# Query-key products added on VectorE before one mask matmul, gate bias and residual put into PSUM by ScalarE

## The chip, the cores and the metric

One core of one Trainium2 chip. A core has TensorE (PE, matrix products out of SBUF into PSUM, eight banks of 512 fp32 per partition), VectorE (DVE), ScalarE (ACT), GpSimd (POOL) and SyncE (SP), each with a queue of its own that runs in order, and DMA engines that move data. The metric is device time in microseconds (us) of one execution, the median of several runs. All matrix operands are bf16.

## What is computed

With S = 2048 tokens and D = 512 features, `xn` is the layernorm of `x`, and the output is `x + A(xn) + B(xn)`:

```python
# A: 32 heads of 16 features; every token looks at 8 keys, 2 tokens apart
q, k, v = split(xn @ wqkv)                       # wqkv [512, 1536]
logits[h,s,w] = sum_d q[h,s,d]*k[h,s-2*w,d] * 16**-0.5   # w = 0..7, masked where s-2w < 0
attn = softmax(logits, over w)
A = concat_h(sum_w attn[h,s,w]*v[h,s-2*w]) @ wo  # wo [512, 512]
# B: gMLP with a spatial gate
z = gelu(xn @ w_in)                              # w_in [512, 1792]
z1, z2 = z[:, :896], layernorm(z[:, 896:])
g = w_sp @ z2 + b_sp[:, None]                    # w_sp [2048, 2048]
B = (z1 * g) @ w_out                             # w_out [896, 512]
```

## The kernel before

The program is a list of tasks. Each names its engine, what it reads and writes, and an estimated duration. A planner (`Plan.schedule`, line 94) then plays the tasks through in estimated time, picks for each engine the task that can begin earliest (and among those within 120 ns the one of better class and earlier place in the list), and so fixes the order of each engine's queue before anything runs. Tasks with `prio=FILL` are of a lower class: they fill gaps. Waits between engines are derived from reads and writes, overlapping buffers included: two names for the same place in the SBUF "arena" wait for each other. On the chip every queue keeps the planned order, whatever the real durations are. A task that must wait holds up all that stands behind it in its queue.

Tokens are taken in 16 blocks of 128 (b) and 4 column groups of 512 (j or tc).

*First stage, up to about 78 us of the profile.* `ln_block` (623) normalises a block and transposes it into `xnT`, by PE for the first four and by DMA on SP for the others. `z2_block` (826) makes the second half of z with a gelu on ACT; `z2_sq` and `z2_wave` normalise it (a power on POOL, line 880, and four multiplies on DVE, 883). `v_block` (669) makes the values, which POOL's DMA writes to a scratch tensor in device memory. `qk_pair` (686, matmuls at 694) makes Q and K, transposed, 128 features by 512 tokens, for one of four chunks c of features: chunk c holds features 128c to 128c+127, that is eight heads of 16. ACT copies both out of PSUM (702).

*Attention weights.* `prod_reduce` (713) is called for each j and c. DVE multiplies Q with the eight shifted views of K (720) into a product buffer of 128 x 4096, one of four. After the fourth chunk, 32 matmuls (733) with a 0/1 mask `E8` as stationary operand add up the 16 features of every head. Each uses 32 of the 128 columns of the array, so four run side by side in different column groups, and the four chunks are accumulated in PSUM (banks 6 and 7, `psl`). The mask has 128 columns, 32 for each chunk, and is made on POOL by one memset and eight selects (542 to 550). `softmax` (755) takes maximum and difference out of PSUM on DVE (763, 765) and, after every second j, an exponential on ACT (782) for two j; `softmax_tail` (787) does sums, reciprocal and transposes on DVE.

*z1.* `z1_group` (845, matmuls at 851) makes the first half of z, 28 groups, with a gelu on ACT (856), into `z1T`.

*Gate.* `g_group(fc, tc)` (947) takes one of 7 chunks of 128 features and one tc: 16 matmuls (956) with the transposed spatial weights `wT`, in one of four banks. DVE then adds the bias (963, PSUM to `tg` in SBUF) and multiplies `z1T` by the result in place (966). The spatial weights come in by a transposing DMA on SP (`ld_wT`, 888), in two slots of 2 MB: the one for tc = 0 after the first stage, that for tc = 1 only after the first two value loads (1058), the others when a slot is free.

*Values.* `pv_block(b)` (971): DVE multiplies the gathered values by the attention weights (999, 128 x 4096) and adds eight terms down to one in three steps (1001, 1004, 1007). The result lies in one of two buffers `On`, and a transposing DMA on SP (1010) puts it into `OT`. The values come from the scratch tensor through ACT's queue (983) into two buffers `Ve`.

*Output.* `out_block(tb)` (1016): four matmuls with `wo` (1031) and seven with `w_out` (1035) into one of banks 4 to 7; DVE adds the residual (1041), which ACT's queue has loaded (1022); ACT's queue stores the result (1045). The last block is cut into 384 and 128 columns.

The outer loop (1052) lists, for every tc, the gate groups, the value blocks, and the output blocks of tc - 1.

In the arena, `OT` has a place of its own; `Ve`, the product tiles `Vs`, `On`, `xres` (residual) and `yout` all lie over Q, K and the product buffers; the two `wT` slots lie over input, Q, K and V weights and the V buffers.

Of the kernel before, what the change touches and what calls it, by code (L numbers as in the profile page):

```python
# [14 lines left out]
class Plan:  # L15
# [276 lines left out]
ALU = mybir.AluOpType  # L292
# [11 lines left out]
    fill=1,  # L304
# [5 lines left out]
def build_kernel(nc, A_x, A_wqkv, A_wo, B_x, B_w_in, B_w_sp, B_b_sp, B_w_out, out, report=False, sched_kw=None,  # L310
# [33 lines left out]
    NPB = 4 if R2 else 2  # L344
# [9 lines left out]
    base += 4 * S  # L354
# [5 lines left out]
    off["tg"] = base + FC * 512 + 2048  # L360
# [5 lines left out]
    g3_a = 4 * 512 * NQ + ksz + NPB * 4096  # L366
    off["Ve"] = base
    off["Vs"] = base + (9216 if VEXT else 0)
    off["On"] = off["Vs"] + NVS * 4096
    off["xres"] = off["On"] + 1024  # L370
    off["yout"] = off["xres"] + 2048
    base += max(g3_a, off["yout"] + 2048 - base)
# [22 lines left out]
    with ExitStack() as es:  # L395
# [46 lines left out]
        for s_ in range(2):  # L442
            R1(("On", s_), "On", 512, 512 * s_)
            R1(("tg", s_), "tg", 512, 512 * s_)
# [78 lines left out]
        def setup_masks():  # L523
# [17 lines left out]
            else:  # L541
                T("pool", lambda g: g.memset(A("E8", 128), 1.0), reads=[("rstd", 3)], writes=["E8"], est=150, name="E8a", prio=2)
                for c in range(4):
                    eo = AC(off["E8"] + 32 * c, [[1, 32]])
                    T("pool", (lambda eo, c: lambda g: g.affine_select(
                        out=eo, in_=eo, pattern=[[-16, 32]], compare_op=ALU.is_ge, fill=0.0, base=128 * c,
                        channel_multiplier=1))(eo, c), writes=["E8"], est=250, name="E8b%d" % c, prio=2)
                    T("pool", (lambda eo, c: lambda g: g.affine_select(
                        out=eo, in_=eo, pattern=[[16, 32]], compare_op=ALU.is_ge, fill=0.0, base=15 - 128 * c,
                        channel_multiplier=-1))(eo, c), writes=["E8"], est=250, name="E8c%d" % c, prio=2)  # L550
# [135 lines left out]
        def qk_pair(j, c):  # L686
            k = next_pair()
            for which in range(2):
                col0 = which * 512 + 128 * c

                def mm(t, col0=col0, which=which):
                    last = None
                    for dc in range(4):
                        last = t.matmul(bank(k + which), AC(off["wqk"] + 1024 * dc + col0, [[1, 128]]),  # L694
                                        AC(off["xnT"] + dc * S + 512 * j, [[1, 512]]), start=(dc == 0),
                                        stop=(dc == 3))
                    return last
# [13 lines left out]
        pb_ctr = [0]  # L711

        def prod_reduce(j, c):
            s_ = pb_ctr[0] % NPB
            pb_ctr[0] += 1
            qb = AC(q_off(c, j), [[0, 8], [1, 512]])
            kb = AC(k_off(c, j), [[-2, 8], [1, 512]])
            pbv = AC(off["pb"] + 4096 * s_, [[512, 8], [1, 512]])
            rd = [("QT", c, j), ("KT", c, j), ("KT", c, j - 1) if j > 0 and not R2 else ("KTpad", c, j)]
            T("dve", lambda v: v.tensor_tensor(pbv, qb, kb, ALU.mult), reads=rd, writes=[("pb", s_)],  # L720
              est=c_dve(4096, 2.0), name="prod%d_%d" % (j, c), prio=FILL)

            if R2:
                if c < 3:
                    return

                def mm(t):
                    last = None
                    for wh in range(2):
                        for cc in range(4):  # L730
                            sc = (s_ - 3 + cc) % NPB
                            for g in range(4):
                                last = t.matmul(  # L733
                                    PC(32 * g * PR + 3072 + 512 * wh, [[1, 512]], 32),
                                    AC(off["E8"] + 32 * cc, [[1, 32]]),
                                    AC(off["pb"] + 4096 * sc + 2048 * wh + 128 * g, [[512, 4], [1, 128]]),
                                    start=(cc == 0), stop=(cc == 3))
                    return last
                T("pe", mm, reads=[("pb", i) for i in range(4)] + ["E8"], writes=["psl"],
                  est=8 * 232.0 + 190, name="red%d" % j, margin=cfg.get("m_red", 800.0))  # L740
                return

            def mm(t):
                last = None
                for blk in range(4):
                    t0, ts = tok(4 * j + blk)
                    for w in range(8):
                        last = t.matmul(ps[:, 3072 + blk * 256 + w * 32 + 8 * c: 3072 + blk * 256 + w * 32 + 8 * c + 8],
                                        AC(off["pb"] + 4096 * s_ + 512 * w + t0 - 512 * j, [[ts, 128]]), E8,
                                        start=True, stop=True)  # L750
                return last
            T("pe", mm, reads=[("pb", s_), "E8"], writes=["psl"], est=32 * 25 + 30, name="red%d_%d" % (j, c),
# [141 lines left out]
        for j in range(NJ):  # L894
# [24 lines left out]
            for c in range(4):  # L919
                prod_reduce(j, c)  # L920
# [7 lines left out]
        ld_wT(0)  # L928
        for j in range(NJ):
# [17 lines left out]
        def g_group(fc, tc):  # L947
            k = gcnt[0] % 4
            ts_ = gcnt[0] % 2
            gcnt[0] += 1  # L950
            r_ = tc % NWS

            def mm(t):
                last = None
                for sh in range(NB):
                    last = t.matmul(bank(k), AC(off["z2"] + FH * sh + 128 * fc, [[1, 128]]),  # L956
                                    AC(off["wT"] + WSL * r_ + sh * 512, [[1, 512]]), start=(sh == 0),
# [4 lines left out]
            tgv = A("tg", 512, 512 * ts_)  # L962
# [155 lines left out]
```

## Time and profile before

| | us |
|---|---|
| median of 3 runs | 245.22 (245.14 to 245.85) |
| profiled execution, span of the trace | 243.8 |
| profiled execution, time by the clock of the runs | not given beside the span; the median lies 1.4 above it |
| busy: PE / DVE / ACT / POOL | 237.3 / 198.2 / 85.8 / 40.6 |
| gate matmuls, line 956 | 96.8 (448 weight loads) |
| mask matmuls, line 733 | 7.6 (128 matmuls) |
| products on DVE, line 720 | 36.0 (16) |
| bias add, line 963 / gate multiply, line 966 | 19.1 / 11.9 (28 each) |
| residual add, line 1041 | 11.1 (17) |

The profile is of one execution. Busy time counts an engine's work, not its waits. A group of instructions is a line, an engine and an operation, with the mean duration of one. The chain of work that ended last is followed back from the last instruction, at each step to what released it. PE's matmuls are pipelined: one of 512 columns lasts 379 ns from its start, but the next begins 215 ns after it.

### The profile page before, as it was taken

How to read it: one execution, taken by the hardware profiler on the slowest of the kernel's cores; microseconds unless marked ns; L12 is line 12 of the kernel's file. 1: busy time of each engine (PE TensorE's matmuls, PEld its weight loads, DVE VectorE, ACT ScalarE, POOL GpSimd, SP SyncE). 2: the span in 40 equal slices, each digit the busy share in tenths (PEclk: the TensorE clock that was granted, in tenths of full speed). 3: DMA queues.
4: the chain of work that ended last, by engine and by line, in shares of the span. 5: the costliest groups of instructions: out<-in, count | busy, mean ns of one | idle time of the engine just before them, and what ended most of it. 6: DMA issues, size and time to landing. Idle time of an engine off the chain costs nothing.

```text
span 243.8 us, 3164 instructions
## 1 busy us (share of the span) xinstructions
PE 237.3 (97%) x1203; PEld 110.5 (45%) x1223; DVE 198.2 (81%) x274; ACT 85.8 (35%) x167; POOL 40.6 (17%) x74
## 2 busy tenths in 40 slices
PE   7999999999999999999999999999999999999995
PEld 2444444444445444444444444454444544444543
DVE  4696877885989868649999994699999999999932
ACT  2798468968999896624000000000000000000000
POOL 4555947360340022000000000000000000000000
PEclk9999999999999999999999999999999999999999
DMA  6999990100109400079984999499771647301352
GB/s 211 362 313 140 201 192 10 67 22 0 67 22 253 92 3 0 0 233 358 227 197 75 270 242 226 77 217 310 225 215 24 210 127 211 82 18 22 100 137 65
DMA packets 70126, 35.47 MB, mean 146 GB/s; under 512 B 49616, under 2 KB 69472, under 8 KB 70112
## 3 DMA queue, kind: packets, MB, share of 16 engines
q1 hardware_dynamic: 53856, 18.29, 36.3%
q10 hardware_dynamic: 15456, 14.88, 20.1%
q0 software_dynamic: 800, 2.11, 3.0%
q8 instruction: 9, 0.15, 0.2%
q14 instruction: 5, 0.04, 0.1%
HBM read 19.01 MB, written 4.21 MB: 95 GB/s over the span
## 4 chain that ended last, share of the span: by engine, by line
PE 88%; DMA 5%; ACT 2%; issue 2%; POOL 1%; ACTq 1%; DVE 0%; DVEq 0%; POOLq 0%
PE ps L956 39%; PE ps L834 10%; PE ps L851 10%; PE ps L1035 10%; PE ps L694 7%; PE ps L1031 6%; PE ps L733 3%; PE ps L676 3%; DMA vscr<-arena 3%; DMA arena<-in_B_w_in_dram 2%; ACT arena L702 1%; POOL vscr L683 0%; ACT arena L680 0%; ACT arena L782 0%; POOL fpool L632 0%
## 5 line engine op out<-in xcount | busy, mean ns | idle before, releaser
L956 PE MATMUL ps<-arena 128*128 128x512 bf16 x440 | 96.8, 379 | 0.4
L956 PEld LDWEIGHTS ps<-arena 128*128 128x128 bf16 x448 | 43.8, 98 | 52.8
L999 DVE TENSOR_TENSOR arena<-arena 128x4096 bf16<-128x4096 bf16 x16 | 36.6, 2285 | 2.5 <-DMA arena<-vscr 2.5
L720 DVE TENSOR_TENSOR arena<-arena 128x4096 bf16<-128x4096 bf16 x16 | 36.0, 2284 | 0.0
L694 PE MATMUL ps<-arena 128*128 128x512 bf16 x127 | 28.2, 379 | 0.6 <-ACT arena L680 0.5
L1035 PE MATMUL ps<-arena 128*128 128x512 bf16 (+2 forms) x117 | 26.9, 366 | 0.1
L834 PE MATMUL ps<-arena 128*128 128x448 bf16 x128 | 25.6, 353 | 0.5 <-DMA arena<-in_B_w_in_dram 0.2
L851 PE MATMUL ps<-arena 128*128 128x512 bf16 x108 | 24.0, 379 | 0.4 <-issue 0.3
L963 DVE TENSOR_TENSOR arena<-ps,arena 128x512 bf16<-128x512 f32 x28 | 19.1, 683 | 1.1 <-PE ps L956 0.9
L694 PEld LDWEIGHTS ps<-arena 128*128 128x128 bf16 x128 | 12.4, 98 | 15.9 <-ACT arena L680 1.0
L1001 DVE TENSOR_TENSOR arena<-arena 128x2048 bf16<-128x2048 bf16 x16 | 19.5, 1217 | 0.0
L856 ACT ACTIVATE arena<-ps 128x512 bf16<-128x512 f32 x28 | 16.4, 598 | 7.5 <-PE ps L851 7.3
L839 ACT ACTIVATE arena<-ps 128x448 bf16<-128x448 f32 x32 | 17.2, 547 | 3.3 <-PE ps L834 1.4
L1035 PEld LDWEIGHTS ps<-arena 128*128 128x128 bf16 x119 | 13.1, 113 | 11.4
L702 ACT ACTIVATE arena<-ps 128x1024 bf16<-128x1024 f32 x16 | 16.0, 1021 | 5.9 <-PE ps L694 5.6
L834 PEld LDWEIGHTS ps<-arena 128*128 128x128 bf16 x128 | 12.0, 98 | 13.1 <-issue 0.6
L851 PEld LDWEIGHTS ps<-arena 128*128 128x128 bf16 x112 | 10.8, 98 | 13.6 <-issue 0.8
L1041 DVE TENSOR_TENSOR arena<-ps,arena 128x512 bf16<-128x512 f32 (+2 forms) x17 | 11.1, 655 | 7.0 <-PE ps L1035 7.0
L1031 PE MATMUL ps<-arena 128*128 128x512 bf16 (+2 forms) x66 | 16.5, 366 | 0.1
L861 ACT ACTIVATE arena<-arena 128x896 bf16<-128x896 bf16 x16 | 15.1, 945 | 0.2
L676 PE MATMUL ps<-arena 128*128 128x512 bf16 x61 | 13.8, 379 | 0.3 <-issue 0.2
L880 POOL TENSOR_TENSOR fpool<-fpool 128x4 f32<-128x4 f32 x4 | 10.1, 2518 | 20.7 <-DVE fpool L877 20.7
(60 smaller groups left out, 180.5 us busy)
## 6 DMA issues: line engine op xcount, KB each, us to landing
arena<-vscr ACTq DMA_DIRECT2D x8, 1152.0 KB, 7.4
arena<-in_A_x_dram ACTq DMA_DIRECT2D x18, 128.0 KB, 4.6
vscr<-arena POOLq DMA_DIRECT2D x16, 128.0 KB, 2.1
out_dram<-arena ACTq DMA_DIRECT2D x15, 128.0 KB, 2.1
arena<-in_A_x_dram SPq DMA_DIRECT2D x14, 128.0 KB, 7.2
arena<-in_A_wqkv_dram SPq DMA_DIRECT2D x2, 512.0 KB, 8.0
arena<-in_B_w_in_dram SPq DMA_DIRECT2D x1, 896.0 KB, 8.2
arena<-in_B_w_out_dram SPq DMA_DIRECT2D x1, 896.0 KB, 11.4
```

What stands on the lines that cost most here:

```text
L676: last = t.matmul(bank(k), AC(off["xnT"] + dc * S + 128 * b, [[1, 128]]), AC(off["wv_raw"] + 512 * dc, [[1, 512]]), start=(dc == 0), stop= ...
L694: last = t.matmul(bank(k + which), AC(off["wqk"] + 1024 * dc + col0, [[1, 128]]), AC(off["xnT"] + dc * S + 512 * j, [[1, 512]]), start=(dc ...
L702: T("act", lambda a: a.activation(AC(qo, [[ko - qo, 2], [1, 512]]), ps[:, 512 * k: 512 * k + 1024].rearrange("p (t n) -> p t n", t=2), ACT ...
L720: T("dve", lambda v: v.tensor_tensor(pbv, qb, kb, ALU.mult), reads=rd, writes=[("pb", s_)], est=c_dve(4096, 2.0), name="prod%d_%d" % (j, c ...
L834: last = t.matmul(ps[:, 512 * k: 512 * k + HF], AC(off["xnT"] + dc * S + 128 * b, [[1, 128]]), AC(off["w_in"] + 1792 * dc + c0, [[1, HF]]) ...
L851: lastm = t.matmul(bank(k), AC(off["w_in"] + 1792 * dc + 128 * fc, [[1, 128]]), AC(off["xnT"] + dc * S + 512 * j, [[1, 512]]), start=(dc = ...
L956: last = t.matmul(bank(k), AC(off["z2"] + FH * sh + 128 * fc, [[1, 128]]), AC(off["wT"] + WSL * r_ + sh * 512, [[1, 512]]), start=(sh == 0 ...
L963: T("dve", lambda v: v.tensor_tensor(tgv, bank(k), A("bbc", 512, 512 * tc), ALU.add), reads=[("ps", k), "bbc"], writes=[("tg", ts_)], est= ...
L999: T("dve", lambda v: v.tensor_tensor(tv, iv, av, ALU.mult), reads=[("attn", j)] + rdv, writes=[("Vs", sv)], est=c_dve(4096, 2.0), name="pv ...
L1001: T("dve", lambda v: v.tensor_tensor(A("Vs", 2048, 4096 * sv), A("Vs", 2048, 4096 * sv), A("Vs", 2048, 4096 * sv + 2048), ALU.add), writes ...
L1031: t.matmul(po, AC(off["OT"] + 512 * tb + 128 * cc, [[1, 128]]), AC(off["wo"] + 512 * cc + c0, [[1, n]]), start=(cc == 0), stop=False)
L1035: last = t.matmul(po, AC(off["z1T"] + fc * S + t0, [[ts, 128]]), AC(off["w_out"] + 512 * fc + c0, [[1, n]]), start=False, stop=(fc == FC - 1))
```

## The change

- *Products added first.* Chunk c of Q and K now holds features c, c+4, c+8 and so on (the weights are read at every fourth column), so a partition belongs to the same head in all four chunks. DVE adds the four product tensors in place (three additions of 128 x 4096 for each j), and the mask matmul has one chunk instead of four: 8 matmuls instead of 32 for each j. There are three product buffers, whose parts rotate with j. The mask has 32 columns and is made with two selects.
- *Gate bias.* ACT copies the bias row into the bank first, the 16 matmuls add to what is there (`start=False`), and one DVE operation multiplies `z1T` with the bank. `tg` is gone. For tc = 0 the banks come from the ring of six.
- *Residual.* ACT copies the residual into the bank before the output matmuls, and copies the sum out after them.
- *Buffers.* `OT` lies over `xnT`; `Vs` over Q and K; `On`, `xres` and `yout` over the product buffers; `Ve` has a place of its own.
- *Spatial weights.* The load for tc = 1 stands directly behind that for tc = 0.

```diff
-    NPB = 4 if R2 else 2
+    NPB = 3
...
     off["OT"] = base
-    base += 4 * S
     off["xnT"] = base
...
-    off["tg"] = base + FC * 512 + 2048
...
-    off["Ve"] = base
-    off["Vs"] = base + (9216 if VEXT else 0)
-    off["On"] = off["Vs"] + NVS * 4096
+    off["Vs"] = off["QT"]
+    off["On"] = off["pb"]
     off["xres"] = off["On"] + 1024
     off["yout"] = off["xres"] + 2048
-    base += max(g3_a, off["yout"] + 2048 - base)
+    base = off["pb"] + NPB * 4096
+    off["Ve"] = base
+    base += 9216
...
-                col0 = which * 512 + 128 * c
+                col0 = which * 512 + c
...
-                        last = t.matmul(bank(k + which), AC(off["wqk"] + 1024 * dc + col0, [[1, 128]]),
+                        last = t.matmul(bank(k + which), AC(off["wqk"] + 1024 * dc + col0, [[4, 128]]),
...
+        def prod_reduce(j):
+            pa, pb, pc = [(j + i) % NPB for i in range(3)]
...
+            def psum(a, b, n):
+                T("dve", lambda v: v.tensor_tensor(A("pb", 4096, 4096 * a), A("pb", 4096, 4096 * a),
+                                                   A("pb", 4096, 4096 * b), ALU.add),
+                  reads=[("pb", b)], writes=[("pb", a)], est=c_dve(4096, 2.0), name="padd%d_%d" % (j, n), prio=FILL)
+
+            prod(0, pa)
+            prod(1, pb)
+            psum(pa, pb, 0)
+            prod(2, pb)
+            prod(3, pc)
+            psum(pb, pc, 1)
+            psum(pa, pb, 2)
 
             def mm(t):
                 last = None
...
+                for wh in range(2):
+                    for g in range(4):
+                        last = t.matmul(PC(32 * g * PR + 3072 + 512 * wh, [[1, 512]], 32), A("E8", 32),
+                                        AC(off["pb"] + 4096 * pa + 2048 * wh + 128 * g, [[512, 4], [1, 128]]),
                                         start=True, stop=True)
                 return last
...
+            T("pe", mm, reads=[("pb", pa), "E8"], writes=["psl"], est=2 * 232.0 + 190, name="red%d" % j,
...
         ld_wT(0)
+        ld_wT(1)
...
         def g_group(fc, tc):
-            k = gcnt[0] % 4
-            ts_ = gcnt[0] % 2
+            k = next_bank() if tc == 0 else gcnt[0] % 4
...
+            T("act", lambda a: a.activation(bank(k), A("bbc", 512, 512 * tc), ACTF.Copy), reads=["bbc"],
+              writes=[("ps", k)], est=c_act(512), name="gs%d_%d" % (fc, tc))
...
-                                    AC(off["wT"] + WSL * r_ + sh * 512, [[1, 512]]), start=(sh == 0),
+                                    AC(off["wT"] + WSL * r_ + sh * 512, [[1, 512]]), start=False, skip_group_check=True,
...
-            T("dve", lambda v: v.tensor_tensor(tgv, bank(k), A("bbc", 512, 512 * tc), ALU.add),
-              reads=[("ps", k), "bbc"], writes=[("tg", ts_)], est=c_dve(512) + 20, name="gb%d_%d" % (fc, tc))
...
-            T("dve", lambda v: v.tensor_tensor(uv, tgv, uv, ALU.mult), reads=[("tg", ts_)],
-              writes=[("z1T", fc, tc)], est=c_dve(512, 2.0) + 30, name="u%d_%d" % (fc, tc))
+            T("dve", lambda v: v.tensor_tensor(uv, bank(k), uv, ALU.mult), reads=[("ps", k)],
+              writes=[("z1T", fc, tc)], est=c_dve(512) + 20, name="u%d_%d" % (fc, tc))
...
+                T("act", (lambda c0, po, n: lambda a: a.activation(po, A("xres", n, 512 * sx + c0), ACTF.Copy))(c0, po, n),
+                  reads=[("xres", sx)], writes=[("ps", k)], est=c_act(n), name="os%d_%d" % (tb, p_))
...
-                T("dve", (lambda c0, po, n: lambda v: v.tensor_tensor(A("yout", n, 512 * sx + c0), po,
-                                                                     A("xres", n, 512 * sx + c0), ALU.add))(c0, po, n),
...
+                T("act", (lambda c0, po, n: lambda a: a.activation(A("yout", n, 512 * sx + c0), po, ACTF.Copy))(c0, po, n),
...
-                if tc == 0 and q == 1:
-                    ld_wT(1, after=[("Ve", 0), ("Ve", 1)] if VEXT else [("Vs", 1)])
```

## The prediction

> **What bounds the kernel now.** I read the busy table first, then the chain of work that ended last, then a table of busy time by stage, and only then single rows of engines. The page opens with TensorE (PE) at 97% of the span:
>
> ```profile
> PE 237.3 (97%) x1203; PEld 110.5 (45%) x1223; DVE 198.2 (81%) x274; ACT 85.8 (35%) x167; POOL 40.6 (17%) x74
> PE 88%; DMA 5%; ACT 2%; issue 2%; POOL 1%; ACTq 1%; DVE 0%; DVEq 0%; POOLq 0%
> ```
>
> The second line, shares of the chain by engine, says the same: what ended last is matrix work laid end to end. The chain in order of time (start, length, what) shows where the part that the change touches lies in it:
>
> ```profile
> 41.51 1.84 PE ps L733 x32
> 43.35 0.16 issue
> ...
> 59.11 1.84 PE ps L733 x32
> ...
> 85.43 1.84 PE ps L733 x32
> ...
> 102.91 1.84 PE ps L733 x32
> 104.75 0.16 issue
> 104.91 1.67 PE ps L851 x7
> 106.59 9.06 PE ps L956 x42
> ```
>
> L733 is the mask matmul that adds up query-key products: four times 1.84 us, every one on the chain, with neighbours that begin as soon as it ends. Time taken from L733 is time taken from the end, if nothing else becomes late. What could become late is VectorE (DVE), which the change gives more work. The table by stage (window, its length, busy us of each engine):
>
> ```profile
> 14.00:41.40 27.40, 26.76 (x127) 12.22 (x126) 21.78 (x43) 20.77 (x40) 18.60 (x27) 1.00 0.86 166
> 41.40:78.50 37.10, 36.77 (x223) 17.11 (x226) 30.25 (x39) 32.99 (x67) 11.78 (x14) 1.00 0.24 65
> 78.50:106.40 27.90, 27.48 (x173) 12.20 (x175) 20.58 (x22) 20.58 (x41) 2.98 (x1) 1.00 0.19 46
> 106.40:154.80 48.40, 48.19 (x222) 21.94 (x225) 38.67 (x53) 3.79 (x3) 0.00 (x0) 1.00 0.97 223
> 154.80:231.00 76.20, 75.83 (x348) 35.83 (x354) 75.33 (x92) 0.00 (x0) 0.00 (x0) 1.00 0.57 143
> ```
>
> Columns after the length are PE, PE weight load, DVE, ACT, POOL, granted clock (1.00 throughout), DMA. PE is idle for 2.0 of these 217.0 us. DVE is idle for 19.8 of 92.4 us before the gate stage (14 to 106.4) and for 10.6 of 124.6 after it. ACT has next to nothing to do from 106.4 on.
>
> **Part 1: the mask matmul.** 32 matmuls of a quarter of the columns take 1.84 us: they run four abreast, eight quartets of 0.23. After the change there are two quartets, 0.46. Saving: 4 x (1.84 - 0.46) = 5.5 us, all on PE's chain. Bounds: a full-width 512 matmul has a cadence of 0.215 (L1035: 1.51 us for 7), so two quartets can't be under 0.43; and if one instruction's own 0.38 us were exposed each time they would be 0.84. The saving is then 4.0 to 5.6. I take 5.5, because the eight quartets together exceed eight full cadences by only 0.12, which leaves little room for a fixed cost. The 0.16 idle after it ("issue") I leave as it is. [...]
>
> **Part 2: Q and K weights read at every fourth column.** 128 weight loads of L694 become strided. The nearest row is L1035, whose stationary operand already has a step of four elements: 113 ns a load against 98 ns for L694 and L956, at an unchanged cadence of 0.215. So 128 x 15 ns = 1.9 us more on the weight loader, hidden under matmuls that are twice as long; 0 on the path, 1.9 if the cover failed. [...]
>
> **Part 3: DVE.** Added: 12 in-place sums of 128x4096, each like the product of the same shape (L720, 2284 ns; L1001 at half the size 1217), 27.4 us. Removed: 28 SBUF multiplies of the gate (L966, 425 ns), 11.9 us, since the multiply now reads PSUM itself at the 683 ns that L963 took; and 17 residual adds (L1041), 11.1 us. Net +4.4, but unevenly: all 27.4 fall before the gate stage, where DVE has 19.8 idle, so some 8 us or more of products, sums and softmax spill past 106; the relief falls behind it. Over 14 to 231 the idle time was 30.4; it becomes 30.4 - 27.4 + 11.9 + 8.2 (12 of the adds lie there) - 5.5 (a shorter span) = 17.6 us. Waits that go: those for L733, 9.7 us, since only one of three product buffers is held by the matmul where all four were, and 2.5 us for the value load. Waits that stay by the row: GpSimd's power (2.8), two buffers for O behind the SP queue (5.3 at L1007), the early layernorm waits. If no other wait goes, 18.2 us of them meet 17.6 of room up to 225.5, and 22 up to 230, the time by which the last O must be done: the last output block begins at 238.7 now (233.2 then), and O's transpose takes 2.8 to land. It fits by some 4 us, so I cost DVE at nothing: PE has work that needs no attention result (z1, gate groups) to lie over its lateness. Cover gone, every us of DVE past that is paid at the end, where the last output blocks wait for the last transposed O (the last L1007 ends at 231.0 now).
>
> **Part 4: bias and residual through ACT.** 28 copies of 512 into PSUM and 17 pairs of copy in and copy out. No row shows ACT writing PSUM; L856 out of PSUM took 598 ns, L861 within SBUF 945 for 896 elements, which less 384 elements at the slope between L839 (448 elements, 547) and L856 (0.8 ns each) is 0.64 for 512. Either way some 62 x 0.6 = 37 us on an engine idle for 130. A gate group's copy needs its bank free four groups earlier and a group lasts 16 x 0.215 = 3.45 us, so the copy is done two groups ahead; residual copies have four banks likewise. 0 on the path. Cover gone (copy after matmul after copy), 45 x 0.6 = 27 us. New waits: ACT now waits for DVE's multiply before each gate copy and for the output matmul before each copy out, and behind these stand its own DMA issues (value reload, residual load, stores; 0.34 to 0.46 us each). A value reload that waits for DVE holds up later gate copies; PE feels it only past some 7 us. I take +0.3 for this and for the exponential (L782: table 1.28 and 1.91), which comes later because DVE does, into the stretch where ACT must empty a bank every 0.86 us. Ends: 0, and one such block unabsorbed, 3.2.
>
> **Part 5: buffers and queues.** O shares the place of the normalised input, so its transposes wait for the last z1 (106.4); the first was issued at 128.9, so nothing waits. The two product tiles of the values lie on Q and K: the first may begin after the last product, which moves from about 101 to about 115. The value buffers are free from the start, so their first two loads can leave ACT's queue 60 us sooner (2 x 0.37 us of issue); DMA is at 0.00 share from 50 to 60. The second spatial-weight transpose goes from 116.5, behind the first output weight, to directly behind the first one (72.2, 7.5 us of issue), and SP has nothing else to send before 106.6. GpSimd saves six selects of 0.28 at 10 to 11.7, which PE doesn't wait for. Ends: a gain of 0.5 (PE's one wait of 0.54 at 32.7, for a value write queued behind GpSimd) and a loss of 3, if early value loads slow those writes. I take 0.
>
> **Part 6: the end.** Both last copies out now share ACT with the stores: about 0.49 and 0.28 instead of 0.56 and 0.29, with one store issue of 0.4 between them. +0.2, between -0.2 and +0.6.
>
> Sum: -5.5 + 0.3 + 0.2 = -5.0. The profiled execution's span of 243.8 becomes 238.8; its own time isn't given beside the span, but the runs' median of 245.22 lies 1.4 above it, so 240.2.
>
> **Rivals.** *A, DVE late (slower side):* the place is the last output blocks waiting for L1007. For it: DVE was 99% busy from 154.8 to 231, and O's transposes stood behind a spatial-weight transpose on SP for up to 13.9 us. Against: the relief of 20 us lies in that very stretch. If all 18 us of its old waits stay and the first stage loses another 10 to 13, 6 to 9 are left over beyond the 4 of room: 246 to 249. It begins to cost once the last L1007 ends past about 230, and past 235 the kernel is slower than before. A milder lateness gives 241 to 244. *B, ACT in order:* one blocked copy per gate column, 1 to 3 us in all, 241.5 to 243; the exponential's 3.2 us and ACT's 33.0 of 37.1 busy before 78.5 speak for it, six banks in the ring against. *C, the mask matmul saves less:* 4.0 of saving, 241.7; if two quartets cost what eight do, 245.5, against which the 0.23 a quartet speaks. *D, more gained:* if PE's other waits of 2.0 us vanish too, 238.2.
>
> **Chances.** My forecast (239.3 to 240.9) 0.50; D 0.08; C and B and mild A, all still faster, 0.23; A in full 0.13; no change 0.03, other losses 0.03. A measurement of this kernel tells about 0.3% from no change (0.7 us). Faster 0.81, same 0.03, slower 0.16. The range, 238.4 to 244.5, leaves out most of A and little of D.
>
> **What would show it.** L733 at 32 matmuls and about 0.5 us each on the chain; PE still without a gap from 14 to the end; a DVE group of 12 at 2.28 us; L966's group gone; no PE idle time put down to ACT copies or to O's transpose. Wrong would be: PE idle before L1031 or L1035, released by DMA of O, or before L956, released by ACT.

## The result, and the profile after

The changed kernel takes 241.44 us (median of 4 runs, 241.30 to 242.56), the kernel before 245.48 (4 runs, 245.14 to 245.85): a ratio of 0.985, with a 95% interval of 0.982 to 0.988. That is 4.0 us faster; 240.2 was predicted. The profiled execution took 241.3 us and its span is 239.6 (before: span 243.8).

The page of the changed kernel, busy time by engine, and the shares of the chain that ended last:

```profile
PE 232.3 (97%) x1107; PEld 109.8 (46%) x1127; DVE 204.1 (85%) x241; ACT 118.5 (49%) x227; POOL 41.6 (17%) x68
PE 89%; DMA 7%; DVE 1%; ACTq 1%; issue 1%; ACT 0%
```

PE is still 97% busy, in 5 us less; ACT has 33 us more to do, DVE 6. The chain is still PE's, with more DMA in it than before. The same chain in order of time (start, length, what) shows what was bought and what was paid:

```profile
48.14 0.55 PE ps L735 x8
...
70.19 0.54 PE ps L735 x8
...
94.38 0.55 PE ps L735 x8
...
124.38 0.55 PE ps L735 x8
...
147.57 4.48 DMA arena<-arena
152.05 0.05 issue
152.10 1.04 PE ps L1019 x4
153.13 1.51 PE ps L1023 x7
154.64 3.47 PE ps L944 x16
158.11 7.39 DMA arena<-arena
165.50 0.05 issue
165.55 1.04 PE ps L1019 x4
```

L735 is the mask matmul (L733 before): 0.55 us for 8 matmuls instead of 1.84 for 32. The two DMA steps are new. They are transposes of O (L995), and PE waits for them at 152.10 and 165.55 before the `wo` matmuls (L1019) of an output block. PE's waits give their sum, number and longest:

```profile
PE ps L1019 <- DMA arena<-arena: 1.1, 2, 0.5
```

The two O came late for different reasons, which are to be read off two queues. SP's queue (start, time to issue, what; for several in a row the time runs from the first start to the last end):

```profile
141.35 7.41 SPq L995 DMA_TRANSPOSE arena<-arena  x2
...
149.24 8.83 SPq L877 DMA_TRANSPOSE arena<-in_B_w_sp_dram  x1
158.11 66.84 SPq L995 DMA_TRANSPOSE arena<-arena  x14
```

and DVE's timeline, with the last additions of the second and the third value block:

```profile
145.79 0.69 DVE L951 TENSOR_TENSOR arena<-ps,arena 128x512 bf16<-128x512 f32 x1 [0.53 <-PE ps L944]
...
147.11 0.42 DVE L992 TENSOR_TENSOR arena<-arena 128x512 bf16<-128x512 bf16 x1
...
152.23 0.42 DVE L992 TENSOR_TENSOR arena<-arena 128x512 bf16<-128x512 bf16 x1
```

For the first wait nothing stood in the way on SP: the sum was ready at 147.53, its transpose left at 147.57 and landed 4.48 us later (the quickest in this profile took 2.4), half a microsecond after PE was ready. DVE had itself stood idle for 0.53 us before it, for PE, with a gate multiply ahead of O's last additions in its queue. The second wait is another matter. The sum was ready at 152.65, but SP was still issuing the 2 MB transpose of spatial weights, from 149.24 to 158.07. O's transpose, a small one, stood behind it, left at 158.11 and landed 7.39 us later, at 165.50; PE began the block at 165.55. The table by stage (window, length, busy us of PE, weight load, DVE, ACT and POOL, granted clock, DMA) has the rest:

```profile
14.00:41.40 27.40, 27.24 (x129) 13.64 (x131) 23.54 (x44) 21.11 (x43) 17.30 (x26) 1.00 0.99 223
41.40:78.50 37.10, 36.94 (x188) 18.04 (x190) 35.30 (x36) 33.14 (x73) 15.35 (x16) 1.00 0.49 113
78.50:106.40 27.90, 27.79 (x134) 12.40 (x135) 26.76 (x22) 22.81 (x39) 2.98 (x1) 1.00 0.42 106
106.40:154.80 48.40, 47.62 (x223) 21.54 (x227) 46.18 (x55) 12.14 (x20) 0.00 (x0) 1.00 0.56 125
154.80:231.00 76.20, 75.28 (x345) 35.35 (x350) 64.40 (x66) 19.64 (x34) 0.00 (x0) 1.00 0.63 151
```

DVE is now nearly full from 41 to 155 (108.2 of 113.4 us) and has 11.8 us free behind it, where it had almost none: the work moved forward, as the prediction had it. PE's gaps have moved from the first stages into the last two. The groups (busy, mean ns, idle time before and what ended it) give each new operation its price:

```profile
L719 DVE TENSOR_TENSOR arena<-arena 128x4096 bf16<-128x4096 bf16 x12 | 27.4, 2286 | 0.2
...
L951 DVE TENSOR_TENSOR arena<-ps,arena 128x512 bf16<-128x512 f32 x28 | 19.1, 681 | 4.7 <-PE ps L944 4.6
...
L938 ACT ACTIVATE ps<-arena 128x512 f32<-128x512 bf16 x28 | 16.6, 600 | 60.5 <-DVE arena L951 60.4
...
L690 PEld LDWEIGHTS ps<-arena 128*128 128x128 bf16 x128 | 14.3, 113 | 13.6 <-ACT arena L676 0.5 <-ACT arena L848 0.4
```

Twelve sums at 2.29 us, a gate multiply that reads PSUM at 0.68, an ACT copy into PSUM at 0.60, Q and K weight loads at 113 ns: the four durations that the prediction took from neighbouring rows agree with it within 1% (for the ACT copy it had two, 0.60 and 0.64; the first was right).

**Where 4.2 us of span went.** PE's last matmul ended at 241.29 before and ends at 236.97 now, 4.32 earlier; what follows it took 0.1 longer.

| us | |
|---|---|
| mask matmuls: 4 x 1.84 = 7.36 became 0.55 + 0.54 + 0.55 + 0.55 = 2.19 | -5.17 |
| the "issue" gaps of 0.16 behind three of them, gone | -0.48 |
| PE's wait of 0.54 for a value bank at 32.7, gone | -0.54 |
| first Q and K matmul begins later (`w_in` landed later) | +0.25 |
| waits for O, 0.52 and 0.55, and the four matmuls behind each 1.04 instead of 0.86 | +1.43 |
| not assigned | +0.2 |
| PE's end | -4.3 |

### The profile page after: what moved, and what is told of

Its sections match the earlier page's. It is cut to its first block, busy times and chain, and to the rows that moved or that the text cites. A ratio compares the mean times of both kernels' runs of the same rounds, so it can differ in the third digit from the quotient of the medians.

```text
span 239.6 us, 2997 instructions
## 1 busy us (share of the span) xinstructions
PE 232.3 (97%) x1107; PEld 109.8 (46%) x1127; DVE 204.1 (85%) x241; ACT 118.5 (49%) x227; POOL 41.6 (17%) x68
## 4 chain that ended last, share of the span: by engine, by line
PE 89%; DMA 7%; DVE 1%; ACTq 1%; issue 1%; ACT 0%
PE ps L944 36%; PE ps L690 12%; PE ps L838 10%; PE ps L821 10%; PE ps L1023 9%; PE ps L672 6%; PE ps L1019 5%; DMA arena<-arena 5%; DMA arena<-in_B_w_in_dram 2%; PE ps L735 1%; ACTq L559 0%; ACT arena L1029 0%; DVE arena L951 0%; DVE arena L989 0%; ACTq L569 0%
## 5 line engine op out<-in xcount | busy, mean ns | idle before, releaser
L944 PE MATMUL ps<-arena 128*128 128x512 bf16 x439 | 97.2, 379 | 0.5
L944 PEld LDWEIGHTS ps<-arena 128*128 128x128 bf16 x448 | 43.8, 98 | 52.9 <-issue 0.4
L938 ACT ACTIVATE ps<-arena 128x512 f32<-128x512 bf16 x28 | 16.6, 600 | 60.5 <-DVE arena L951 60.4
L984 DVE TENSOR_TENSOR arena<-arena 128x4096 bf16<-128x4096 bf16 x16 | 36.5, 2283 | 0.0
L714 DVE TENSOR_TENSOR arena<-arena 128x4096 bf16<-128x4096 bf16 x16 | 36.2, 2284 | 0.2
L690 PE MATMUL ps<-arena 128*128 128x512 bf16 x126 | 28.4, 379 | 0.1
L719 DVE TENSOR_TENSOR arena<-arena 128x4096 bf16<-128x4096 bf16 x12 | 27.4, 2286 | 0.2
L1029 ACT ACTIVATE arena<-ps 128x512 bf16<-128x512 f32 (+2 forms) x17 | 9.7, 572 | 30.2 <-PE ps L1023 30.2
L838 PE MATMUL ps<-arena 128*128 128x512 bf16 x109 | 24.2, 379 | 0.2
L951 DVE TENSOR_TENSOR arena<-ps,arena 128x512 bf16<-128x512 f32 x28 | 19.1, 681 | 4.7 <-PE ps L944 4.6
L690 PEld LDWEIGHTS ps<-arena 128*128 128x128 bf16 x128 | 14.3, 113 | 13.6 <-ACT arena L676 0.5
L1023 PEld LDWEIGHTS ps<-arena 128*128 128x128 bf16 x119 | 13.1, 113 | 11.4
L821 PEld LDWEIGHTS ps<-arena 128*128 128x128 bf16 x128 | 12.2, 98 | 12.9 <-DMA arena<-in_B_w_in_dram 0.8
L1019 PE MATMUL ps<-arena 128*128 128x512 bf16 (+2 forms) x66 | 16.4, 366 | 1.1 <-DMA arena<-arena 1.1
L838 PEld LDWEIGHTS ps<-arena 128*128 128x128 bf16 x112 | 10.9, 98 | 13.4 <-issue 0.4
```

The lines of the kernel that those rows point to most:

```text
L719: T("dve", lambda v: v.tensor_tensor(A("pb", 4096, 4096 * a), A("pb", 4096, 4096 * a), A("pb", 4096, 4096 * b), ALU.add), reads=[("pb", b) ...
L821: last = t.matmul(ps[:, 512 * k: 512 * k + HF], AC(off["xnT"] + dc * S + 128 * b, [[1, 128]]), AC(off["w_in"] + 1792 * dc + c0, [[1, HF]]) ...
L838: lastm = t.matmul(bank(k), AC(off["w_in"] + 1792 * dc + 128 * fc, [[1, 128]]), AC(off["xnT"] + dc * S + 512 * j, [[1, 512]]), start=(dc = ...
L951: T("dve", lambda v: v.tensor_tensor(uv, bank(k), uv, ALU.mult), reads=[("ps", k)], writes=[("z1T", fc, tc)], est=c_dve(512) + 20, name="u ...
L984: T("dve", lambda v: v.tensor_tensor(tv, iv, av, ALU.mult), reads=[("attn", j)] + rdv, writes=[("Vs", sv)], est=c_dve(4096, 2.0), name="pv ...
L1019: t.matmul(po, AC(off["OT"] + 512 * tb + 128 * cc, [[1, 128]]), AC(off["wo"] + 512 * cc + c0, [[1, n]]), start=False, stop=False, skip_gro ...
```

## The experiments

Two things had to be told apart. The first theory (M in the expectations) says that the gain is PE's alone: what the shorter mask matmul frees, and that every other part only makes room for it. Against it stand the theories (rival L) that one of the other parts brings something by itself: the relief of DVE by ACT, the new buffers with the earlier weight load, or the end of some wait. The second matter was the +1.4 us of waits for O: a lateness of DVE, as in rival A, or something that stands in the way of O on SP's queue. The kernel before, timed beside them, took 245.22 with the first four and 245.34 with the other eight. Every edit also makes the planner lay out the queues anew, so a run can differ from its base in more than its edit; the traces show where.

**Mask matmul at its old length.** In the changed kernel, the same 8 matmuls are issued four times over, so that PE has 32 again; the sums on DVE stay.

```diff
-                    for g in range(4):
-                        last = t.matmul(...)
+                    for rep in range(4):
+                        for g in range(4):
+                            last = t.matmul(...)
...
-            T("pe", mm, ..., est=2 * 232.0 + 190,
+            T("pe", mm, ..., est=8 * 232.0 + 190,
```

> The changed kernel with every mask matmul issued four times (32 for each j again, each overwriting the same sums), the additions on VectorE kept. Theory M (PE is the bound, and the gain is PE time that the mask matmul no longer takes): the four groups grow from 0.55 to 1.84 us, so the time grows by 4 x 1.29 = 5.2 and lies at 246.2 to 247.2, above the kernel before. Rival L (the gain comes from the buffers, from waits that went, or from the work taken off VectorE): PE's extra time is absorbed, 241.4 to 242.5.

Measured: 253.65 us (252.75 to 254.06), ratio 1.034 (1.031 to 1.037). A miss: 12.2 us above the changed kernel, where the mask alone explains 5. PE's timeline (in brackets the idle time before, and what ended it) shows one wait that neither theory had expected:

```profile
181.24 1.89 PE L1020 MATMUL ps<-arena 128*128 128x512 bf16 x4 [5.73 <-DMA arena<-arena]
```

SP's queue in this run:

```profile
154.61 20.70 SPq L878 DMA_TRANSPOSE arena<-in_B_w_sp_dram  x1
```

The transposing load took SP 20.7 us here, against 8.8, and O's transpose behind it came out only then. The stage table around the wait:

```profile
175.40:181.20 5.80, 0.11 (x1) 0.00 (x0) 0.00 (x0) 0.00 (x0) 0.00 (x0) 0.92 1.16 265
181.20:185.90 4.70, 4.66 (x11) 1.60 (x12) 4.64 (x5) 0.60 (x1) 0.00 (x0) 0.50 0.28 72
```

After 5.7 us without work PE ran at a clock of 0.50 in this row. Its output block took 4.67 us, from 181.24 to the gate groups at 185.91, where the others of this run take 2.38, and the first 48 gate matmuls 11.12, where the slope of its other rows (20.88 for 96, 13.98 for 64) gives 10.5: some 2.9 us are lost. So 4.7 (this wait less the changed kernel's 1.07) + 2.9 + some 5 for the mask make about the 12.7 by which the spans differ (252.3 against 239.6). This run doesn't tell how much the mask is worth, but it tells what the output blocks hang on: on where O's transpose stands against the weight load on SP.

**The sums alone.** The changed kernel with bias, gate multiply and residual back on DVE; the buffers stay.

```diff
-            T("act", lambda a: a.activation(bank(k), A("bbc", ...), ACTF.Copy), ... name="gs...")
+            T("dve", lambda v: v.tensor_tensor(tgv, bank(k), A("bbc", ...), ALU.add), ... name="gb...")
...
-            T("dve", lambda v: v.tensor_tensor(uv, bank(k), uv, ALU.mult), ...)
+            T("dve", lambda v: v.tensor_tensor(uv, tgv, uv, ALU.mult), ...)
...
-                T("act", ... a.activation(po, A("xres", n, 512 * sx + c0), ACTF.Copy) ... name="os...")
...
-                T("act", ... a.activation(A("yout", ...), po, ACTF.Copy) ... name="fin...")
+                T("dve", ... v.tensor_tensor(A("yout", ...), po, A("xres", ...), ALU.add) ... name="fin...")
```

> The changed kernel with bias add, gate multiply and residual add on VectorE as before, so only the additions, the mask matmul and the new buffers are left of the change. Theory M alone (VectorE has room whatever it does): 241.4 within 0.7. Theory M with VectorE near its limit: VectorE gets back 11.9 + 11.1 us of work, of which 20 lie before the last output blocks; its last sum ended at 223.3 and has 7 us of room there and some 6 us of idle time earlier, so about 7 us are left over: 244 to 249, with PE waiting for the transposed O ahead of the last output blocks.

Measured: 256.99, 260.62, 261.74 and 262.59 us; the ratio, from the two shorter runs, is 1.056 (1.047 to 1.065), that is 13.6 us above the kernel before. A miss: the higher forecast was 244 to 249. DVE is busy 226.1 us instead of 204.1, and PE's waits say where it is paid:

```profile
PE ps L1019 <- DMA arena<-arena: 14.0, 5, 4.4
```

Four of these waits, 9.6 us together, stand before the last output blocks; the last O was summed only at about 251. The fifth, of 4.35 us, comes at 172.95: O's transpose stood behind a weight load that held SP from 149.79 to 166.37. And PE was slower behind three of them (the granted clock was 0.50 from 235.32 to 238.00 and 0.974 over the run): by the starts of its groups, against 2.38 us for an output block elsewhere in this run, that cost some 1.7, 2.8 and 1.7 us, 6.2 in all. The 14.0 less the changed kernel's 1.07, and 6.2, make 19.1, the difference of the spans (258.8 of the run of 260.62, against 239.6). The forecast had counted the overflow of DVE alone, neither the queue of SP nor the clock. Without ACT's help DVE sets the end, and the sums alone turn a gain of 4 into a loss of some 14; how much of it is DVE's, the run with the output blocks later, below, tells.

**ACT's part alone.** The kernel before, with bias and residual through ACT and nothing else.

```diff
+            T("act", lambda a: a.activation(bank(k), A("bbc", 512, 512 * tc), ACTF.Copy), ... name="gs...")
...
-            T("dve", ... tgv, bank(k), A("bbc", ...), ALU.add ...)
-            T("dve", ... uv, tgv, uv, ALU.mult ...)
+            T("dve", ... uv, bank(k), uv, ALU.mult ...)
...
-                T("dve", ... A("yout", ...), po, A("xres", ...), ALU.add ...)
+                T("act", ... A("yout", ...), po, ACTF.Copy ...)
```

> The kernel before with only bias and residual moved to ScalarE; products, mask matmuls and buffers as before. Theory M: VectorE is relieved by 23 us, but PE is the bound and keeps all its work, so 245.5 within 0.7. Rival L: 1 to 3 us faster, 242.5 to 244.5.

Measured: 246.98, 247.01, 255.14 and 259.38 us, the last two at a mean granted clock of 0.987 and 0.980. Runs that lie 12 us apart give no verdict. The profile is of the one of 247.01; its PE timeline names a candidate:

```profile
130.98 2.33 PE L957 MATMUL ps<-arena 128*128 128x512 bf16 x10 [0.69 <-DMA arena<-in_B_w_sp_dram]
```

PE, now ahead of the old order, reached the gate groups of the next tc before their spatial weights: the load was issued at 118.17 and took 12.76 us to land. In the kernel before that load stands behind the first two value loads. That the two longer runs had a longer wait at this place, with the clock lowered behind it, is only a guess from one profile; whether the load makes the scatter, the run with the load moved up, below, tests.

**Buffers alone.** The kernel before with the new places of `OT`, `Vs`, `On` and `Ve`, and with the second load of spatial weights directly behind the first.

```diff
+    off["Vs"] = off["QT"]
+    off["On"] = off["pb"]
...
+    base = off["pb"] + NPB * 4096
+    off["Ve"] = base
...
         ld_wT(0)
+        ld_wT(1)
```

> The kernel before with only the buffers laid out anew (OT over xnT, value buffers of their own) and the second spatial weight load moved up. Theory M: at most PE's one wait of 0.54 us goes, 244.7 to 245.7. Rival L: it gives most of the 4 us, 241.5 to 243.

Measured: 246.01 us (245.74 to 246.26), ratio 1.003 (1.002 to 1.005): 0.8 us slower, not faster, and 0.3 above the forecast of M. In the profile PE ends at 240.77, 0.5 earlier than before, because the wait of 0.54 for the value bank is gone; but the last store of 32 KB landed 2.6 us after its issue instead of 1.6; why, no run shows. What follows: the buffers bring half a microsecond to PE at most, and nothing to the time.

**Output blocks planned later.** The planner counts an output block as ready some time after its inputs, a margin of 300 ns by default (L1028). Here it is 8000, so that PE is given gate groups first and the output blocks come later. Nothing is added or taken away.

```diff
+    m_out=8000.0,
```

> The changed kernel, with the planner told to keep 8 us between the planned arrival of what an output block needs and its start (before 0.3), so that gate groups come first. In the changed kernel PE waited 0.52 and 0.55 us for a transposed O that stood behind a spatial-weight transpose on SP. If these waits are what separates the result from the forecast: 240.0 to 240.8. If something else ends last there: 241.4 within 0.4.

Measured: 239.94 us (239.48 to 240.90), ratio 0.979 (0.976 to 0.981). The window from 14 to 231:

```profile
14.00:231.00 217.00, 217.00 (x1040) 102.03 (x1039) 197.40 (x222) 110.16 (x207) 36.14 (x44) 1.00 0.61 142
```

PE is busy for 217.00 of 217.00 us. The transposing load still stands on SP's queue:

```profile
142.36 7.41 SPq L996 DMA_TRANSPOSE arena<-arena  x2
150.25 8.79 SPq L878 DMA_TRANSPOSE arena<-in_B_w_sp_dram  x1
159.09 65.16 SPq L996 DMA_TRANSPOSE arena<-arena  x14
```

and DVE does the same work. All that changed is that PE has something else to do until O is there. So the +1.4 were an order of work, not a shortage of an engine. No run moved the weight load on SP, so its part in the second wait is read from the trace, not tested. This kernel is the fastest of the study. (The head of this profile has a wait of 1.8 us for `w_in`, against 0.7 in the changed kernel's, which is why the spans, 239.2 and 239.6, are nearer than the medians.)

**Q and K weights contiguous again.** The changed kernel with 128 neighbouring columns in each weight load; so a partition holds features of four different heads in the four chunks, the additions mix them, and the logits are others, while every instruction keeps its size.

```diff
-                col0 = which * 512 + c
+                col0 = which * 512 + 128 * c
...
-                        ... AC(off["wqk"] + 1024 * dc + col0, [[4, 128]]),
+                        ... AC(off["wqk"] + 1024 * dc + col0, [[1, 128]]),
```

> The changed kernel with Q and K weights read in contiguous columns again, so that every addition mixes heads and the sums are not the reference's; everything else is equal. If the strided weight loads lie under the matmuls: 241.4 within 0.4, and the loads of that line at 98 ns instead of 113. If they are on PE's path: up to 1.9 us faster, 239.5.

Measured: 241.27 us (240.65 to 241.70), ratio 0.984 (0.981 to 0.985), the same as the changed kernel. The loads of this run (least, median and greatest ns):

```profile
L690 PEld LDWEIGHTS ps<-arena x128: 95/98/99, 13.3 to 67.7; 128*128 128x128 bf16 x128
```

98 ns instead of 113, and no difference in time: 15 ns a load lie under the matmuls.

**More work for DVE.** The changed kernel with the fourth product computed a second time for each j: four multiplies of 2.28 us, 9.1 us more on DVE and nothing else.

```diff
             prod(3, pc)
+            prod(3, pc)
```

> The changed kernel with the fourth product of every j computed twice: 9.1 us more on VectorE ahead of the gate stage, nothing more on PE. If VectorE has the room that the trace shows (its last sum ended at 223.3, the last output block began at 234.4, a transpose takes 3 to 4, and some idle time lies before): 241.4 to 242.5. If VectorE already sets the end: 248 to 250.5.

Measured: 241.15 us (240.77 to 241.64), ratio 0.983 (0.981 to 0.985). It costs nothing. The last sum begins at

```profile
231.08 0.43 DVE L993 TENSOR_TENSOR arena<-arena 128x512 bf16<-128x512 bf16 x1
```

which is 7.8 us later than in the changed kernel (223.31), and PE waits 1.36 us before the last output block, about what it waited for O elsewhere in the changed kernel. Those two earlier waits are gone in this plan, which is luck: against the kernel without any wait for O (239.94) the 9 us cost 1.2. The room was just used up.

**Twice that.** The fourth product three times, 18.3 us more on DVE.

```diff
             prod(3, pc)
+            prod(3, pc)
+            prod(3, pc)
```

> The same with that product computed three times: 18.3 us more on VectorE. With 7 us of room at the end and some 6 of idle time before, 5 are left over: 244 to 249. If VectorE has far more room: under 242.5.

Measured: 251.63 us (251.20 to 252.36), ratio 1.025 (1.023 to 1.028), above the forecast of 244 to 249. The last sum and PE's waits:

```profile
242.40 0.42 DVE L994 TENSOR_TENSOR arena<-arena 128x512 bf16<-128x512 bf16 x1
```

```profile
PE ps L1021 <- DMA arena<-arena: 8.8, 4, 4.6
```

The second 9 us cost 10.5. Between the two runs DVE becomes the bound, as rival A described it: at the last output blocks, once the last sum ends later than some 231. Of the 10.5, 7.4 are waits for O (8.8 less 1.36); after the longest of them, 4.63 us, PE's clock was 0.50 from 230.41 to 233.00, and its block took 4.01 us instead of the next one's 2.37, some 1.6 lost; and in this profile PE's first wait for `w_in` was 1.0 longer.

**The mask again, with the output blocks later.** The first experiment and the planner's margin of 8000 together: the mask has its old length where no output block waits for O.

```diff
+    m_out=8000.0,
...
+                    for rep in range(4):
```

> The changed kernel with the mask matmuls issued four times, as in the first run of this kind, and output blocks kept 8 us from the planned arrival of O. That first run came out 7 us above its forecast, and its trace holds one wait of 5.73 us for O with PE's clock at 0.57 to 0.68 after it. If theory M is right and only that wait was in the way: 239.9 + 5.2, that is 244.6 to 245.9, level with the kernel before. If more mask matmuls cost more than their PE time: above 247. Rival L: under 242.

Measured: 245.07 us (244.76 to 246.00, 10 runs), ratio 0.999 (0.998 to 1.001). Its mask group:

```profile
L737 PE MATMUL ps<-arena 128*32 128x512 bf16 x128 | 7.6, 380 | 0.0
```

PE waits for no O here. Against 239.94 with 8 matmuls, the 32 cost 5.13 us, and they take the kernel back to the time of before (245.34, and 245.12 with its output blocks later). Where no output block waits for O, the shorter mask matmul is the whole gain; this is the run that shows it.

**ACT's part alone, with the early weight load.** The third experiment with the load of spatial weights for tc = 1 moved up.

```diff
         ld_wT(0)
+        ld_wT(1)
...
-                if tc == 0 and q == 1:
-                    ld_wT(1, after=[("Ve", 0), ("Ve", 1)] if VEXT else [("Vs", 1)])
```

> The kernel before with bias and residual on ScalarE, and the second spatial weight load moved up behind the first, buffers as before. Without that move the time scattered from 247 to 259, and the trace showed PE's 0.7 us wait for that load. If the scatter came from that load: 245.3 within 0.7, runs close together. If it comes from ScalarE's part itself: 247 or more, with scatter.

Measured: 245.89 us (245.24 to 246.23, 10 runs), ratio 1.001 (1.000 to 1.003). The scatter of 12 us is gone with the late load, so the load had made it; how, no trace of a longer run shows. And relief of DVE by 21 us (busy 177.3 instead of 198.2, in the profile of ACT's part alone) is worth nothing while PE is the bound. The moved load, which looks like a detail of the change, is what the ACT part needs.

**The sums alone, with the output blocks later.** All edits of the second experiment, and the planner's margin.

```diff
+    m_out=8000.0,
...
-            T("act", lambda a: a.activation(bank(k), A("bbc", ...), ACTF.Copy), ... name="gs...")
+            T("dve", lambda v: v.tensor_tensor(tgv, bank(k), A("bbc", ...), ALU.add), ... name="gb...")
```

> The changed kernel with bias and residual on VectorE as before, and output blocks kept 8 us from the planned arrival of O. Without that spacing it took 261. If VectorE's work sets the end: its 226 us of work can't end much before 245, so 250 to 256, with PE waiting for O ahead of the last blocks whatever the spacing. If only the order of the output blocks was unlucky: 240 to 243.

Measured: 254.84 us (252.96 to 256.11), ratio 1.038 (1.032 to 1.043). PE's waits:

```profile
PE ps L1020 <- DMA arena<-arena: 10.7, 5, 3.0
```

All of these come after 226; the wait behind SP's weight load is gone. The better order wins back some 4 us (258.8 was the middle of the two shorter runs), but 15 us of loss against the same order with ACT's part (239.94) remain. The last sum began at 242.51 here: a late engine can't be ordered away.

**The kernel before, with the output blocks later.**

```diff
+    m_out=8000.0,
```

> The kernel before with output blocks kept 8 us from the planned arrival of O, and nothing else. Its PE waits for no O, so nothing can be won: 245.3 within 0.6. If the spacing helps by itself: 244 or less.

Measured: 245.12 us (244.82 to 246.33), ratio 1.000 (0.999 to 1.001). Nothing: in the kernel before no output block waited for O, so the order had nothing to give.

Put together, in us against the kernel before:

| | usual order | output blocks later |
|---|---|---|
| nothing | 0 | -0.2 |
| sums on DVE, short mask, buffers, without ACT's part | +13.6 | +9.5 |
| ACT's part (early weight load) | +0.6 | not tried |
| the whole change | -4.0 | -5.4 |
| the whole change, mask at its old length | +8.4 | -0.3 |

## Why the prediction was right

The sign and the mechanism were right, the time was forecast 1.2 us too low: outside the likeliest case's own range (239.3 to 240.9), where the prediction had put mild A (241 to 244), and close to C's 241.7, though the mask saved what was forecast. That the time came so near is in part luck: terms that went wrong by -1.1 and by +1.9 in all partly cancel. By its steps:

- *Part 1, the mask matmul (-5.5).* 5.17 measured in the chain and 5.13 by experiment (245.07 against 239.94). The size was 0.3 too large: 8 matmuls take 0.55, not 0.46. Two lengths give the two terms: 1.84 - 0.55 = 1.29 for six quartets is 0.215 each, the plain cadence, and so 0.12 is left as a fixed cost of each group. The prediction had seen that 0.12 ("exceed eight full cadences by only 0.12") and then divided it among the quartets. What it had left as it was, the 0.16 behind the group, went three times out of three (-0.48; with the 32 matmuls again, in the run of the mask with the output blocks later, two such gaps are back), so that the whole came out at 5.65. (By the prediction's own sum, rival C without any saving should read 245.7, not 245.5.)
- *Part 2, strided weights (0).* Right: 113 ns as its row said, and 241.27 without the stride against 241.44 with it.
- *Part 3, DVE (0).* The price list was right to the row, and DVE never became the bound at the end. The room was misjudged: the prediction allowed "some 4 us" and a last sum by 230; the last sum ended at 223.73, and the experiments put the room between 9 and 18 us, near the 9. The prediction let DVE's 5.3 us wait for the O buffers and its 2.8 for GpSimd stand; in the profile after the first has gone and the second is 1.8.
- *Part 4, ACT (+0.3).* No wait of PE is put down to ACT in this profile; the term is 0. ACT's 33 us are hidden. Rival B falls.
- *Part 5, buffers and queues (0).* Here is the step that failed. The value-bank wait of 0.54 went (the bound of a gain of 0.5, which the prediction named and did not take). In its place came 1.43 for two late O, one of the signs that the prediction had named as wrong: PE idle before L1031 (now L1019), released by the DMA of O. The first O was late by its own sum and transpose, the second by the spatial-weight transpose on SP. The prediction knew this second mechanism and its price range: it had noted "up to 13.9 us" of it in the kernel before, as evidence for rival A. But it looked for late O at the last output blocks, where DVE's lateness would show, and not at the first ones of tc = 0, where the third value block's sum ends just after SP has begun to issue the last of the four transposing loads. Moving the output blocks back took both waits away and gained 1.5, which shows that the waits were the cost; what made each O late is read from the trace.
- *Part 6, the end (+0.2).* +0.1.

The sum of the terms: -0.15 for the mask with its gaps, -0.3 for ACT, -0.54 for the value bank, +0.25 for the start, +1.43 for O, -0.1 for the end and +0.2 unassigned are +0.8, which makes -5.0 into the -4.2 of the span. The other 0.4 lies outside it: the profiled time was 1.7 above the span, not 1.4, and the median 0.14 above the profiled time. Rival A's threshold was a last sum that ends at about 230; the runs with more DVE work agree with it (no cost with an end at 231.51, 10.5 us at 242.82) and with its place, and show that the change stayed about 9 us of DVE work clear of it. What the prediction didn't say, and what the experiments make plain, is how much the parts need each other: the sums without ACT's part lose some 14 us, ACT's part without the early weight load scatters over 12, and ACT's part by itself is worth nothing.

## What to carry to other kernels

A gain on the bounding engine is worth its own row, but only if the engine that pays for it has room up to the moment its last result is needed: work that out as a time, and count the relief that the change brings along as part of the price, not as a second gain. Wherever a small transfer shares an in-order queue with a large one, look for every place where the two can meet, not only the last; where they met here (O's transpose, 1.19 us to issue, behind a load that held SP for 8.83), giving the waiting engine other work first cost nothing. And when a single part of a change is tried alone, take along the queue order that it relies on, or the experiment measures that instead.

## What the runs showed of the hardware

After some of the waits for O, PE's granted clock was 0.50, and the wait so cost more than its length. In the run of the sums alone with the output blocks later, PE's timeline has, among others,

```profile
226.53 1.04 PE L1020 MATMUL ps<-arena 128*128 128x512 bf16 x4 [3.04 <-DMA arena<-arena]
...
235.32 1.86 PE L1020 MATMUL ps<-arena 128*128 128x512 bf16 x4 [2.82 <-DMA arena<-arena]
```

and the stage table behind these two waits, with the columns as above (the granted clock stands behind POOL):

```profile
226.53:229.50 2.97, 2.49 (x10) 1.10 (x11) 2.87 (x3) 0.00 (x0) 0.00 (x0) 1.00 0.37 88
...
235.32:238.00 2.68, 2.67 (x7) 0.99 (x8) 2.65 (x5) 0.00 (x0) 0.00 (x0) 0.50 0.13 42
```

The four `wo` matmuls of a block took 1.04 us after the first wait and 1.86 after the second, which was shorter. So the length of a wait alone doesn't decide. All waits of more than 1 us for O before blocks of 512 columns, in the four runs where the clock fell, with the time of the two groups of the block behind each (1.03 and 1.67 us where there was no wait), and the granted clock of windows behind them:

| run | wait, us | four `wo` matmuls | seven `w_out` matmuls | granted clock (from, to) |
|---|---|---|---|---|
| mask at its old length | 5.73 | 1.89 | 3.19 | 0.50 (181.2, 185.9) |
| 18 us more on DVE | 4.63 | 1.86 | 2.51 | 0.50 (230.4, 233.0) |
| 18 us more on DVE | 1.42 | 1.02 | 1.67 | |
| sums alone | 4.35 | 1.15 | 3.19 | |
| sums alone | 3.37 | 1.89 | 3.19 | 0.50 (235.3, 238.0) |
| sums alone | 2.88 | 1.02 | 1.67 | |
| sums alone | 2.43 | 1.62 | | |
| sums alone, output blocks later | 3.04 | 1.04 | 1.67 (six in the trace) | 1.00 (226.5, 229.5) |
| sums alone, output blocks later | 2.82 | 1.86 | 2.50 | 0.50 (235.3, 238.0) |

Before blocks of 384 columns, a wait of 2.17 us (18 us more on DVE) was followed by groups of 0.82 and 1.30, one of 2.98 (sums alone, output blocks later) by groups of 1.46 and 2.12 at a clock of 0.50 (246.0, 248.0). So the shortest wait with slow matmuls behind it is 2.43 us, and the longest without is 3.04; what decides it, no run shows. In the run with 9 us more on DVE (longest wait 1.36 us, groups of 0.82 and 1.30 behind it) the mean clock was 1.00, and in the changed kernel (waits of 0.52 and 0.55) each row of the stage table has 1.00. The price is no trifle: behind the wait of 5.73 us some 2.9 us more were lost.

Issuing one 2 MB transposing load held SP's queue for 7.45 us (18 us more on DVE, at 125.74) to 20.70 (mask at its old length, at 154.61) in these runs; what makes the difference no run shows.
